# Reordered weight-row steps, an earlier value pass and one sink copy per pair in the first leg of a sink-window attention and squared-ReLU feed-forward kernel

## The chip, the core and the metric

The kernel runs on one core of a Trainium2 chip. The metric is the device time of one execution in microseconds (us). A core has TensorE (PE, with its weight loads PEld), VectorE (DVE), ScalarE (ACT), GpSimd (POOL) and SyncE (SP, which here only issues DMA transfers). Each engine works through its own instructions in the order in which they were written into its queue; semaphores make one engine wait for another.

## What is computed

```python
def _attn_ref(q, k, v, n_sink, window):          # 4 batches, 8 heads, 768 positions, head width 64
    scores = np.matmul(q, k.transpose(0, 1, 3, 2)) / np.sqrt(D)
    keep = is_sink | in_window                   # 4 sink keys and the last 128 keys
    scores = np.where(keep, scores, -1e9)
    a = np.exp(scores - scores.max(-1, keepdims=True))
    a = a / (a.sum(-1, keepdims=True) + 1e-9)
    return np.matmul(a, v)

def _moe_ref(x, w_in, w_out):                    # x: 3072 tokens x 512, from the heads above
    h = np.maximum(x @ w_in, 0.0)                # w_in 512 x 2048
    return h * h @ w_out                         # w_out 2048 x 512
```

The weights arrive as 64-bit floats and are split in the kernel into a high and a low part.

## The kernel before

The 3072 tokens are cut into 8 chunks of 384 (`c`), two to a batch. The 8 heads are taken as 4 pairs (`p`), so that a "pair" is one step of attention work for one chunk: `pairs` 0 to 3 belong to chunk 0, 4 to 7 (the fifth to the eighth) to chunk 1. For one pair the work is: `scores` (PE products `s`, a DVE pass at L263 that masks them and finds the maximum, an ACT exponential at L266), `normalise` (POOL, L291 to L305, which also packs the probabilities of the sink keys into `PSK`), `tail` (PE transposes the probabilities into PSUM tiles `pt`, and ACT or DVE copies them to `PTF`, L364 and L366; its middle step `sink_keys` transposes the sink probabilities into `pss` and copies them to `SK`, L325 and L326), and `values` (PE products `xo` from `PTF` and `SK`; ACT and DVE split the result into the high and low part of `x`, L418 and L419).

The feed-forward part (`moe`) runs in legs. For each of the 8 blocks of 128 hidden columns of a half leg it makes 12 products `ph` (L466) in two halves of 6, ACT applies ReLU and squares (L477, L480, L482), DVE forms the low part `gl` (L489), and one block later 9 products `po` follow (L504), three for each of three token tiles. It is written as a generator, and one call of `next(products)` is a quantum: half a block of `ph`, the other half, two thirds of `po`, the last third.

The weights come in 32 rows of 128 x 512 values. A row is loaded by SP into one of four buffers `raw` and then takes five steps in `split_steps`: `t` (DVE L569), a combination of `t` (DVE L571), `m` in two halves (ACT L573 and DVE L574), `eb` (DVE L576), and the two results (ACT L582 and DVE L583). `m`, `eb` and one of the temporaries have a single buffer each. The list `order` sets the order of rows: four rows of `w_in` ("i"), then four of `w_out` ("o"), and so on. A block of `ph` needs the four "i" rows of its quarter, a block of `po` the "o" row of its number.

In the first part of the program all queues are written by hand. There is a first stage (some 36 us) with the attention of the first four pairs and the start of the fifth, and then the first leg: 32 quanta (`QUANTA`), each of which takes one `next(products)`, one entry of the list `todo`, and `fill(k)`, that is k row steps. `todo` holds, for each of the pairs after the fifth, three entries of scores, one of `normalise`, one of `values` for the pair two before it, three steps of the `tail` of the pair before it, and one that loads `v`. The PSUM tiles of scores, `pt` and `pss` in this leg come from one pool of two buffers (`att`), so that each is written only when the one two before it has been read. 17 of the 32 rows are split by the end of the first leg (`EARLY`); the others follow in the second leg.

Of the kernel before, what the change touches and what calls it, by code (L numbers as in the profile page):

```python
# [19 lines left out]
P = 128  # L20
D = 64
NS = 8
# [3 lines left out]
NQ = TOK // P  # L26
WR = 512
SW = 64
# [9 lines left out]
def f32(ap):  # L38
    return ap.bitcast(F32)
# [3 lines left out]
def sink_window_attention_moe(  # L43
# [11 lines left out]
    nc = tc.nc  # L55
    B, NPAIR, _, S = q.shape
    H = 2 * NPAIR
    DM, FF = w_in.shape
    NCC = DM // P
# [9 lines left out]
    with ExitStack() as fast:  # L69
# [37 lines left out]
        ident = wp.tile([P, P], F32, name="ident")  # L107
# [45 lines left out]
        SK = wp.tile([P, TOK], F32R, name="SK")  # L153
# [38 lines left out]
        def load_v(c, p):  # L192
            st = state[c, p]
            st["vn"] = vn = ap2.tile([P, 4, 2, D], F32, tag="vn", name=f"vn_{c}_{p}")
            nc.sync.dma_start(
                out=vn[:, 0 : st["nk"]], in_=v[c // NHALF, p, :, st["kb0"] : st["kb0"] + st["nk"]]
            )
# [33 lines left out]
        def bank(tag, name):  # L231
            pool = {"att": ps_att, "h": ps_h, "xo": ps_x}.get(tag, ps_o)
            return pool.tile([P, 512], F32, tag=tag, name=name)
# [73 lines left out]
        def sink_keys(c, p, tag="att"):  # L307
            n = NQ - (1 if c % NHALF == 0 else 0)
            pss = bank(tag, f"pss_{c}_{p}")
            own = PSK[p % 2 if c < 2 else 0]  # L310
            if c > 1 and n == NQ:
                nc.tensor.transpose(pss[:, 0:P], f32(own[:, 0:2]).rearrange("p a c -> p (a c)"), ident)
                for a in range(NQ):
                    cols = slice(a * P, (a + 1) * P)
                    nc.vector.tensor_copy(SK[0 : 4 * NS, cols], pss[4 * NS * a : 4 * NS * (a + 1), 0:P])
                    nc.scalar.copy(SK[4 * NS : 6 * NS, cols], pss[4 * NS * a : 4 * NS * a + 2 * NS, 0:P])
                return
            for a in range(0, n, 2):
                nc.tensor.transpose(  # L319
                    pss[:, a * SW : a * SW + P], f32(own[:, a : a + 2]).rearrange("p a c -> p (a c)"), ident  # L320
                )
            copy = nc.scalar.copy if c == 1 else nc.vector.tensor_copy
            blocks = lambda t: t.rearrange("p (a c) -> p a c", c=P)
            rows = slice(0, 6 * NS)
            copy(blocks(SK[rows, 0 : n * P])[:, 0:n:2], blocks(pss[rows, 0 : (n + 1) // 2 * P]))  # L325
            copy(SK[rows, P : 2 * P], pss[SW : SW + 6 * NS, 0:P])  # L326

        def banks_of(c, p):

# [92 lines left out]
        pairs = [(c, p) for c in range(NCHUNK) for p in range(NPAIR)]  # L422
# [117 lines left out]
        wout_rows = w_out.bitcast(I32).rearrange("(fc p) e -> p fc e", p=P)  # L540

        order = []
        for fq in range(NFQ):
            order += [("i", fq, cc) for cc in range(NCC)] + [("o", 0, 4 * fq + j) for j in range(4)]
        NROW = len(order)
        HALF = NROW // 2
        AHEAD = 2
# [72 lines left out]
        QUANTA = 4 * FH  # L620
        EARLY = HALF + 1
        with tc.manual_schedule(engines={E.PE, E.DVE, E.Activation, E.Pool, E.SP}):
            steps = row_steps()

            def fill(n):
                for _ in range(n):
                    if len(split) < EARLY:
                        next(steps)
# [11 lines left out]
            def tail(s, spare, own=("att",) * 3):  # L640

                a = pairs[s]
                probs(*a, 0, own[0])
                if s == 0:
                    busy(10)
                yield
                sink_keys(*a, spare)
                probs(*a, 1, own[1])
                yield
                probs(*a, 2, own[2])  # L650
                yield
# [13 lines left out]
            for s in range(NPAIR):  # L665
# [19 lines left out]
                if s > 0:  # L685
                    if s > 1:
                        load_v(*pairs[s])
                    t = tail(s - 1, "o2", (*trios[0], trios[1][0]))
# [10 lines left out]
            s = NPAIR  # L699
# [7 lines left out]
            t = tail(s - 1, "o2", (*trios[0], trios[1][0]))  # L707
# [11 lines left out]
            todo = []  # L719
            for s in range(NPAIR + 1, 2 * NPAIR + 1):  # L720
                if s < 2 * NPAIR:
                    todo += [lambda s=s: (s + 1 < 2 * NPAIR and load_qk(*pairs[s + 1]), scores(s, 0))]
                    todo += [lambda s=s, i=i: scores(s, i) for i in range(1, NQ)]
                    todo += [lambda s=s: normalise(*pairs[s], (0, 1))]
                else:
                    todo += [lambda: values(*pairs[s - 2])]
                if s > NPAIR + 1:
                    todo += [lambda s=s: values(*pairs[s - 2])] if s < 2 * NPAIR else []
                t = tail(s - 1, "att")
                todo += [lambda t=t: next(t)] * 3  # L730
                if s < 2 * NPAIR:
                    todo.append(lambda s=s: load_v(*pairs[s]))
            todo.append(lambda: values(*pairs[2 * NPAIR - 1]))
            for n in range(QUANTA):
                next(products)

                if todo:
                    todo.pop(0)()
                fill(2 if n < QUANTA // 2 or n % 4 == 0 or n >= QUANTA - 12 else 1)
                if n % 4 == 3 and n < QUANTA // 2:  # L740
                    fill(1)
            while len(split) < EARLY:
                next(steps)
            for f in todo:
# [273 lines left out]
```

## Time and profile before

| | us |
|---|---|
| median of 3 runs | 703.43 |
| lowest and highest of them | 703.38, 704.15 |
| time of the profiled execution | 703.99 |
| its span, first to last instruction | 702.1 |
| TensorE busy in the span | 684.5 (97%) |
| VectorE busy | 432.1 (62%) |
| ScalarE busy | 439.1 (63%) |
| GpSimd busy | 226.1 (32%) |
| mean granted TensorE clock, share of full speed | 0.997 |

The shares are averages over stages. TensorE's busy time counts pipelined products from start to modelled end, so a product that waits inside a group can be counted as busy; idle time in a timeline row stands in square brackets, with the engine and line that ended it. In a timeline, the time from one row's start to the next row's start on the same engine is what an instruction costs its queue.

### The profile page before, as it was taken

What the parts mean: (1) busy time and instruction counts of PE and PEld (TensorE: products, weight loads), DVE (VectorE), ACT (ScalarE), POOL (GpSimd) and SP (SyncE); (2) the same over time, 40 slices, a digit from 0 to 9 for tenths busy, and PEclk for the clock granted to TensorE, in tenths of its full rate; (3) what the DMA queues carried; (4) which work ended last, traced back from release to release, by engine and by line L of the source; (5) the groups of instructions that cost most, each with busy time, mean ns of one, the idle gap of its engine ahead of it and who ended that gap; (6) DMA issues with size and microseconds to landing.
All of it is one profiled execution on the core that took longest, in us unless ns stands there. A gap on an engine that the chain in (4) does not pass through costs nothing.

```text
span 702.1 us, 11728 instructions
## 1 busy us (share of the span) xinstructions
PE 684.5 (97%) x3854; PEld 592.0 (84%) x3854; DVE 432.1 (62%) x1185; ACT 439.1 (63%) x1244; POOL 226.1 (32%) x433
## 2 busy tenths in 40 slices
PE   8889999999999999999999999999999999999995
PEld 4567889998888898888889888888888889889994
DVE  8988799835667665565566565666556665542221
ACT  6888887755666776776667777667677554422221
POOL 6664400034454432332342443233244242200000
PEclk9999999999999999999999999999999999999998
DMA  7575466412434333333434432243432210000001
GB/s 240 155 233 186 141 234 208 131 45 64 128 74 140 93 91 107 107 103 92 117 90 140 133 100 69 91 137 96 114 95 81 78 44 16 0 35 12 1 0 49
DMA packets 37027, 71.49 MB, mean 102 GB/s; under 512 B 4384, under 2 KB 14368, under 8 KB 36960
## 3 DMA queue, kind: packets, MB, share of 16 engines
q1 hardware_dynamic: 36816, 70.55, 34.1%
q8 instruction: 32, 0.52, 0.3%
q14 instruction: 35, 0.29, 0.1%
q10 hardware_dynamic: 144, 0.13, 0.1%
HBM read 62.80 MB, written 7.86 MB: 101 GB/s over the span
## 4 chain that ended last, share of the span: by engine, by line
PE 90%; ACT 4%; DVE 2%; issue 1%; POOL 1%; DMA 1%; SPq 0%; DVEq 0%; POOLq 0%; ACTq 0%
PE ph L466 37%; PE po L504 37%; PE xo L407 6%; PE s L259 5%; PE pt L377 2%; PE xo L410 2%; PE s L255 1%; ACT P L266 1%; ACT m L573 1%; PE pt L359 1%; DMA raw<-in_moe_w_in_dram 1%; POOL P L291 1%; ACT PTF L366 1%; DVE ob L527 0%; PE pss L319 0%
## 5 line engine op out<-in xcount | busy, mean ns | idle before, releaser
L466 PE MATMUL ph<-x,wi 128*128 128x384 f32 x1536 | 306.3, 340 | 0.6 <-ACT wi L582 0.4
L466 PEld LDWEIGHTS ph<-x,wi 128*128 128x128 f32 x1536 | 265.1, 188 | 10.3 <-issue 1.4
L504 PE MATMUL po<-wo,gh 128*128 128x512 f32 (+1 forms) x770 | 244.4, 398 | 0.0
L227 POOL TENSOR_TENSOR KS<-kn,KS 128x408 fp32r<-128x408 f32 (+1 forms) x48 | 58.2, 1213 | 320.2 <-ACT KS L226 320.2
L504 PEld LDWEIGHTS po<-wo,gh 128*128 128x128 f32 x770 | 136.0, 188 | 19.1 <-issue 1.6
L504 PE MATMUL po<-wo,gl 128*128 128x512 f32 x385 | 151.6, 394 | 0.0
L266 ACT ACTIVATE P<-P,nbs 128x264 f32<-128x264 f32 (+1 forms) x192 | 94.2, 491 | 75.1 <-DVE nbs L263 74.9
L485 DVE TENSOR_TENSOR ph<-ph,r 128x384 f32<-128x384 f32 x96 | 54.0, 563 | 76.8 <-ACT r L477 76.7
L263 DVE CUSTOM_DVE_ANT_0 P<-s,masks 128x264 f32<-128x264 f32 x160 | 67.2, 430 | 52.7 <-PE s L259 49.4
L291 POOL TENSOR_SCALAR P<-P,rs 128x136 f32<-128x136 f32 (+2 forms) x192 | 85.3, 459 | 31.4 <-DVE rs L280 29.5
L477 ACT ACTIVATE r<-ph 128x384 f32<-128x384 f32 x96 | 46.7, 487 | 77.7 <-PE ph L466 74.9
L489 DVE TENSOR_TENSOR gl<-ph,gh 128x384 fp32r<-128x384 f32 x128 | 71.1, 555 | 25.5 <-ACT ph L482 14.0
L504 PEld LDWEIGHTS po<-wo,gl 128*128 128x128 f32 x385 | 72.2, 188 | 16.0
L229 DVE TENSOR_TENSOR QS<-qn,QS 64x384 fp32r<-64x384 f32 x48 | 44.8, 933 | 24.4 <-ACT QS L228 23.9
L259 PE MATMUL s<-KS,QS 128*128 128x264 f32 (+1 forms) x288 | 57.2, 281 | 0.7 <-DVE nbs L263 0.7
L259 PEld LDWEIGHTS s<-KS,QS 128*128 128x128 f32 x288 | 51.9, 188 | 6.3 <-DVE nbs L263 1.5
L286 POOL TENSOR_TENSOR P<-P 128x256 f32<-128x256 f32 (+1 forms) x48 | 48.1, 1002 | 26.0 <-ACT P L266 25.5
L480 ACT ACTIVATE gh<-r 128x384 fp32r<-128x384 f32 x96 | 50.3, 524 | 2.2
L383 DVE TENSOR_TENSOR PTF<-pt,halves 128x256 f32<-128x256 f32 x96 | 36.2, 419 | 22.5 <-PE pt L377 21.9
L407 PE MATMUL xo<-PTF,vn 128*64 128x256 f32 (+1 forms) x448 | 46.5, 342 | 1.0 <-ACT PTF L366 1.0
L407 PEld LDWEIGHTS xo<-PTF,vn 128*64 128x64 f32 x448 | 31.2, 136 | 18.0 <-issue 9.3
L226 ACT CAST KS<-kn 128x408 fp32r<-128x408 f32 (+1 forms) x48 | 28.3, 589 | 26.7 <-issue 14.2
(107 smaller groups left out, 671.4 us busy)
## 6 DMA issues: line engine op xcount, KB each, us to landing
raw<-in_moe_w_in_dram SPq DMA_DIRECT2D x16, 512.0 KB, 3.8
raw<-in_moe_w_out_dram SPq DMA_DIRECT2D x16, 512.0 KB, 3.6
half<-in_moe_w_in_dram SPq DMA_DIRECT2D x32, 256.0 KB, 3.0
half<-in_moe_w_out_dram SPq DMA_DIRECT2D x32, 256.0 KB, 3.1
kn<-in_k_dram SPq DMA_DIRECT2D x24, 272.0 KB, 4.1
qn<-in_q_dram SPq DMA_DIRECT2D x32, 192.0 KB, 3.7
out_dram<-ob SPq DMA_DIRECT2D x23, 256.0 KB, 2.5
kn<-in_k_dram SPq DMA_DIRECT2D x24, 204.0 KB, 3.5
```

The costliest lines, as they stand in the source:

```text
L227: nc.gpsimd.tensor_tensor(KS[:, 1, 0:nk], st["kn"][:, hh, 0:nk], f32(KS[:, 0, 0:nk]), op=ALU.subtract)
L259: nc.tensor.matmul(ps[:, 0:n], st["QS", hh][:, qcols], flat[:, a, c0 : c0 + n], start=(a == 0), stop=(a == 1))
L263: nc.vector.tensor_tensor_reduce(Pt[:, i, 0:n], ps[:, 0:n], mask[:, 0:n], -SCALE, BIG, ALU.add, ALU.min, nb)
L266: nc.scalar.activation(Pt[:, i, 0:n], Pt[:, i, 0:n], AF.Exp, bias=nb, scale=-1.0, accum_out=sm[:, i : i + 1])
L286: nc.gpsimd.tensor_tensor(Pt[:, j0:NQ, 0:P], Pt[:, j0:NQ, 0:P], Pt[:, j0:NQ, BS:BAND], op=ALU.add)
L291: nc.gpsimd.tensor_scalar(Pt[:, j, 0:n], Pt[:, j, 0:n], rs[:, hh, j : j + 1], 1.0, op0=ALU.mult, op1=ALU.mult)
L407: nc.tensor.matmul(xo[h * D : h * D + D, cols], lhsT, rhs, start=(n == 0), stop=False, skip_group_check=True)
L466: nc.tensor.matmul(ph[:, 0:TOK], wi_at(i, cc, fc), xt[:, cc, :], start=(m == 0), stop=(m == 3 * NCC - 1),)
L480: nc.scalar.activation(gh, r, AF.Square)
L485: nc.vector.tensor_tensor(ph[:, 0:TOK], ph[:, 0:TOK], r, op=ALU.mult)
L489: late = lambda: nc.vector.tensor_tensor(gl, ph[:, 0:TOK], f32(gh), op=ALU.subtract)
L504: nc.tensor.matmul(po[t][:, e], gt[:, ts_], wo[f][:, i, e], start=(f == f0 and j == 0), stop=(f == f1 - 1 and j == 2), skip_group_check=True,)
```

## The change

Four edits. The sink transposes of chunks 0 and 1 are made one per token tile (two for each pair of chunk 0, three for each pair of chunk 1) instead of one per two tiles, and they land side by side in `pss`, so that one copy takes them to `SK` instead of two. The fourth "o" row moves behind the second quarter's four "i" rows in `order`. The load of `v` shares a `todo` entry with the third step of the `tail`, so that the entries behind it come one, two and three quanta earlier, and two empty entries stand ahead of the last `values`. And a table `STEPS` sets the row steps of quanta 2, 3, 6, 7 and 10 to 1, 0, 3, 5 and 3, where they were 2, 3, 2, 3 and 2; their sum, 12, is unchanged. For chunks from 2 on the copies of `sink_keys` are written differently but are the same instructions.

```diff
@@ sink_keys
-            if c > 1 and n == NQ:
+            rows = slice(0, 6 * NS)
+            if c < 2:
+
+                for a in range(n):
+                    nc.tensor.transpose(pss[0:SW, a * P : (a + 1) * P], f32(own[:, a]), ident)
+                (nc.scalar.copy if c == 1 else nc.vector.tensor_copy)(SK[rows, 0 : n * P], pss[rows, 0 : n * P])
+                return
+            if n == NQ:
...
-            for a in range(0, n, 2):
-                nc.tensor.transpose(
-                    pss[:, a * SW : a * SW + P], f32(own[:, a : a + 2]).rearrange("p a c -> p (a c)"), ident
-                )
-            copy = nc.scalar.copy if c == 1 else nc.vector.tensor_copy
...
-            copy(blocks(SK[rows, 0 : n * P])[:, 0:n:2], blocks(pss[rows, 0 : (n + 1) // 2 * P]))
-            copy(SK[rows, P : 2 * P], pss[SW : SW + 6 * NS, 0:P])
+            nc.tensor.transpose(pss[:, 0:P], f32(own[:, 0:2]).rearrange("p a c -> p (a c)"), ident)
+            for a in range(n):
+                nc.vector.tensor_copy(SK[rows, a * P : (a + 1) * P], pss[a * SW : a * SW + 6 * NS, 0:P])
@@ order
-            order += [("i", fq, cc) for cc in range(NCC)] + [("o", 0, 4 * fq + j) for j in range(4)]
+            order += [("i", fq, cc) for cc in range(NCC)]
+            order += [("o", 0, 4 * fq + j) for j in range(-1 if fq == 1 else 0, 3 if fq == 0 else 4)]
@@ first leg
-                todo += [lambda t=t: next(t)] * 3
-                if s < 2 * NPAIR:
-                    todo.append(lambda s=s: load_v(*pairs[s]))
-            todo.append(lambda: values(*pairs[2 * NPAIR - 1]))
+                todo += [lambda t=t: next(t)] * 2
+                todo.append(lambda s=s, t=t: (next(t), s < 2 * NPAIR and load_v(*pairs[s])))
+
+            todo += [lambda: None] * 2 + [lambda: values(*pairs[2 * NPAIR - 1])]
+            STEPS = {2: 1, 3: 0, 6: 3, 7: 5, 10: 3}
...
-                fill(2 if n < QUANTA // 2 or n % 4 == 0 or n >= QUANTA - 12 else 1)
-                if n % 4 == 3 and n < QUANTA // 2:
-                    fill(1)
+
+                fill(STEPS.get(n, 2 + (n % 4 == 3) if n < QUANTA // 2 else 2 if n % 4 == 0 or n >= QUANTA - 12 else 1))
```

On the chip's queues this stands as follows. DVE in the first stage, the tail of the third pair (`x`: the low part of the first pair's output of two pairs before; `SK`, `PTF`: the sink and probability copies; `wi`: a weight row's result), before:

```order
L576 TENSOR_SCALAR eb_460<-t_3_458 128x512
L419 TENSOR_TENSOR x_0_401<-xo_1_486,x_0_400 128x384
L325 CAST SK<-pss_2_506 48x128
L326 CAST SK<-pss_2_506 48x128
L364 COPY PTF_2_1_513<-pt_2_1_510 128x256
L583 SCALAR_TENSOR_TENSOR wi<-m_459,eb_460 128x512
L263 ISA P_0_0_532,nbs<-s_0_0_0_533,masks 128x264
```

and after:

```order
L579 TENSOR_SCALAR eb_460<-t_3_458 128x512
L420 TENSOR_TENSOR x_0_401<-xo_1_486,x_0_400 128x384
L316 CAST SK<-pss_2_506 48x256
L365 COPY PTF_2_1_513<-pt_2_1_510 128x256
L586 SCALAR_TENSOR_TENSOR wi<-m_459,eb_460 128x512
L263 ISA P_0_0_532,nbs<-s_0_0_0_533,masks 128x264
```

One copy has gone from between `x` and the copy to `PTF`; nothing else moved there.

ACT in the first leg, from the last exponentials of the sixth pair (`P_1`) over the tail of the fifth (`PTF_0`, `SK`) and the second feed-forward block (`ph_1`, `gh_1`), before:

```order
L266 ACTIVATE P_1_1_642,sm_1_636<-P_1_1_642,nbs 128x264
L582 CAST wo_687<-t_5_652 128x512
L573 COPY m_707<-raw_650 128x512
L366 COPY PTF_0_0_725<-pt_0_0_720 128x512
L582 CAST wo_728<-t_6_706 128x512
L477 ACTIVATE ph_1_713<-ph_1_713 128x384
L480 ACTIVATE gh_1_740<-ph_1_713 128x384
L482 ACTIVATE ph_1_713<-ph_1_713 128x384
L325 CAST SK<-pss_0_744 48x2x128
L326 CAST SK<-pss_0_744 48x128
L366 COPY PTF_0_1_754<-pt_0_1_749 128x512
L366 COPY PTF_0_2_775<-pt_0_2_770 128x512
```

and after:

```order
L266 ACTIVATE P_1_1_642,sm_1_636<-P_1_1_642,nbs 128x264
L367 COPY PTF_0_0_713<-pt_0_0_708 128x512
L585 CAST wo_715<-t_5_652 128x512
L478 ACTIVATE ph_1_701<-ph_1_701 128x384
L481 ACTIVATE gh_1_731<-ph_1_701 128x384
L483 ACTIVATE ph_1_701<-ph_1_701 128x384
L316 CAST SK<-pss_0_735 48x384
L367 COPY PTF_0_1_745<-pt_0_1_740 128x512
L576 COPY m_721<-raw_650 128x512
L367 COPY PTF_0_2_764<-pt_0_2_759 128x512
L585 CAST wo_769<-t_6_720 128x512
```

The first copy to `PTF` now stands ahead of a row's cast and of the next row's `m`; that `m` stands between the second and the third copy.

DVE from the last step of a row of `w_out` towards the second scores of the seventh pair (`P_2`), before:

```order
L583 SCALAR_TENSOR_TENSOR wo_786<-m_757,eb_758 128x512
L569 TENSOR_SCALAR t_8_791<-raw_731 128x512
L571 SCALAR_TENSOR_TENSOR t_8_791<-raw_731,t_8_791 128x512
L263 ISA P_2_0_809,nbs<-s_2_0_0_810,masks 128x264
L263 ISA nbs 128x1
L263 ISA P_2_1_814,nbs<-s_2_1_0_815,masks 128x264
L263 ISA nbs 128x1
L574 TENSOR_SCALAR m_792<-raw_731 128x512
L576 TENSOR_SCALAR eb_793<-t_8_791 128x512
L263 ISA P_2_0_809,nbs<-s_2_0_1_833,masks 128x264
```

and after:

```order
L586 SCALAR_TENSOR_TENSOR wo_769<-m_721,eb_722 128x512
L572 TENSOR_SCALAR t_7_774<-raw_718 128x512
L490 TENSOR_TENSOR gl_1_732<-ph_1_701,gh_1_731 128x384
L263 ISA P_2_0_788,nbs<-s_2_0_0_789,masks 128x264
L263 ISA nbs 128x1
L263 ISA P_2_1_793,nbs<-s_2_1_0_794,masks 128x264
L263 ISA nbs 128x1
L574 SCALAR_TENSOR_TENSOR t_7_774<-raw_718,t_7_774 128x512
L577 TENSOR_SCALAR m_775<-raw_718 128x512
L579 TENSOR_SCALAR eb_776<-t_7_774 128x512
L586 SCALAR_TENSOR_TENSOR wi<-m_775,eb_776 128x512
L572 TENSOR_SCALAR t_8_806<-raw_772 128x512
```

Between the first and the second scores of the seventh pair stand five row steps, where two stood before; the second scores' pass follows behind the last row shown.

## Rows read from the trace of the kernel before

**Rows 1.** Busy time by stretch: stretch; us, then PE, PEld, DVE, ACT, POOL busy.

```profile
0.00:36.00 36.00, 30.73 (x184) 18.21 (x184) 31.48 (x122) 26.31 (x81) 22.26 (x57) 1.00 0.68 199
...
44.00:94.30 50.30, 47.07 (x282) 36.36 (x281) 43.34 (x105) 42.34 (x99) 20.89 (x32) 1.00 0.56 174
...
131.00:702.10 571.10, 562.49 (x3166) 498.31 (x3164) 314.09 (x859) 335.46 (x993) 177.69 (x334) 1.00 0.29 82
```

**Rows 2.** PE's waits, 36 to 97 us: waiter, releaser, us, times, longest.

```profile
PE pt L359 <- ACT PTF L366: 1.4, 1, 1.4
PE xo L407 <- ACT PTF L366: 0.7, 1, 0.7
PE pt L359 <- ACT SK L326: 0.6, 1, 0.6
...
PE ph L466 <- ACT wi L582: 0.4, 1, 0.4
```

**Rows 3.** DVE's timeline, third pair's tail: start us, us, line, operation [idle before].

```profile
28.23 0.56 DVE L419 TENSOR_TENSOR x<-xo,x 128x384 fp32r<-128x384 f32 x1 [0.29 <-ACT x L418]
28.71 0.27 DVE L325 CAST SK<-pss 48x128 fp32r<-48x128 f32 x1
28.99 0.29 DVE L326 CAST SK<-pss 48x128 fp32r<-48x128 f32 x1
29.31 0.42 DVE L364 COPY PTF<-pt 128x256 f32<-128x256 f32 x1
29.66 0.68 DVE L583 SCALAR_TENSOR_TENSOR wi<-m,eb 128x512 fp32r<-128x512 int32 x1
```

**Rows 4.** PE's timeline at the end of the first stage.

```profile
34.20 1.88 PE L407 MATMUL xo<-PTF,vn 128*64 128x256 f32 x12 [0.31 <-ACT PTF L366]
```

**Rows 5.** ACT's timeline at the tail of the fifth pair.

```profile
44.15 0.60 ACT L582 CAST wo<-t 128x512 fp32r<-128x512 f32 x1
...
45.29 0.56 ACT L366 COPY PTF<-pt 128x512 f32<-128x512 f32 x1
...
46.56 0.47 ACT L477 ACTIVATE ph<-ph 128x384 f32<-128x384 f32 x1
...
47.86 0.37 ACT L325 CAST SK<-pss 48x256 fp32r<-48x256 f32 x1
48.24 0.26 ACT L326 CAST SK<-pss 48x128 fp32r<-48x128 f32 x1
...
49.73 0.80 ACT L573 COPY m<-raw 128x512 uint16<-128x512 uint16 x1
```

**Rows 6.** PE's timeline from the fifth pair's tail to the seventh pair's scores.

```profile
44.12 0.38 PE L319 MATMUL pss<-ident,PSK 128*128 128x128 f32 x2
45.91 0.66 PE L359 MATMUL pt<-ident,P 128*128 128x128 f32 x4 [1.40 <-ACT PTF L366]
46.32 0.71 PE L504 MATMUL po<-wo,gh 128*128 128x512 f32 x2
...
48.55 0.65 PE L359 MATMUL pt<-ident,P 128*128 128x128 f32 x4 [0.60 <-ACT SK L326]
...
50.90 0.71 PE L255 MATMUL s<-kn,qn 64*128 64x264 f32 x4
51.54 1.30 PE L466 MATMUL ph<-x,wi 128*128 128x384 f32 x6
52.78 1.03 PE L255 MATMUL s<-kn,qn 64*128 64x264 f32 x4
```

**Rows 7.** DVE's timeline around the seventh pair's first scores.

```profile
50.56 0.69 DVE L583 SCALAR_TENSOR_TENSOR wo<-m,eb 128x512 fp32r<-128x512 int32 x1 [0.30 <-ACT m L573]
51.17 0.44 DVE L569 TENSOR_SCALAR t<-raw 128x512 int32<-128x512 int32 x1
51.65 0.69 DVE L571 SCALAR_TENSOR_TENSOR t<-raw,t 128x512 int32<-128x512 int32 x1
52.26 0.43 DVE L263 CUSTOM_DVE_ANT_0 P<-s,masks 128x264 f32<-128x264 f32 x1
```

More of the change, by code (lines that the diff above doesn't have):

```diff
@@ L317, in sink_keys @@
                 return
-            for a in range(0, n, 2):
-                nc.tensor.transpose(
-                    pss[:, a * SW : a * SW + P], f32(own[:, a : a + 2]).rearrange("p a c -> p (a c)"), ident
-                )
-            copy = nc.scalar.copy if c == 1 else nc.vector.tensor_copy
-            blocks = lambda t: t.rearrange("p (a c) -> p a c", c=P)
-            rows = slice(0, 6 * NS)
-            copy(blocks(SK[rows, 0 : n * P])[:, 0:n:2], blocks(pss[rows, 0 : (n + 1) // 2 * P]))
-            copy(SK[rows, P : 2 * P], pss[SW : SW + 6 * NS, 0:P])
+            nc.tensor.transpose(pss[:, 0:P], f32(own[:, 0:2]).rearrange("p a c -> p (a c)"), ident)
+            for a in range(n):
+                nc.vector.tensor_copy(SK[rows, a * P : (a + 1) * P], pss[a * SW : a * SW + 6 * NS, 0:P])
         def banks_of(c, p):
```

## The prediction, written before the changed kernel was run

> **What bounds the kernel now.** I read the busy times by stretch first. From 131 us on TensorE (PE) is busy 562.5 of 571.1 us, and nothing in the change touches that part [rows 1]. Room is left in two stretches: in the first stage PE is busy 30.7 of 36 us while DVE is busy 31.5, and in the first leg (44 to 94.3 us) PE is busy 47.1 of 50.3 us with DVE at 43.3 and ACT at 42.3 [rows 1]. So a PE wait taken out of either stretch moves the end by as much, until DVE or ACT is late instead; they have only 7 and 8 us of slack in the leg. Second, I read whom PE waits for in the leg: 1.4 us for the copy to `PTF`, 0.6 for the sink copy, 0.4 for a weight row, 0.7 for a copy to `PTF` ahead of the last `values` [rows 2]. Third, the timelines around those waits. The first two are one place, the tail of the fifth pair: PE's second transposes wait for the first copy to `PTF`, the third for the sink copies [rows 6], and both copies stand on ACT behind row steps and ReLU [rows 5]. A fourth loss shows only as a long group: the seventh pair's second scores take 1.03 us where its first take 0.71 [rows 6], some 0.3.
>
> **One sink copy in the first stage.** The two DVE copies hold the queue from 28.71 to 29.31, 0.60 us, and the copy of 256 columns behind them holds it 0.35 (29.31 to 29.66) [rows 3]. One sink copy of 256 columns should cost that 0.35, so 0.25 goes at each of four pairs. It lies on the path: the `x` step ahead of it waits for ACT, whose work follows from the scores' DVE pass of the same round, and DVE then runs on without a gap through the copy and the row step to the next scores [rows 3]; and the last `values` of the stage takes 1.88 us, since its second product waits for a DVE copy behind the sink copies [rows 4]. The additional transpose costs 0.10 (four of them in 46.32 - 45.91 = 0.41 us [rows 6]); at the first pair it stands ahead of the copy and takes 0.1 of the gain, later DVE's wait for `x` hides it. Upper bound 4 x 0.25 = 1.0, lower 0 (if ACT or POOL, which I haven't followed here, set the pace). I take **-0.8**, near the top, because DVE is the busiest engine of the stage [rows 1].
>
> The Trainium skill (VectorE: DVE Perf Modes, the errata section) gives 120 + columns cycles at 0.96 GHz for a PSUM copy, by which two copies of 128 make 0.52 us and one of 256 0.39, and the term would be near -0.4; the rows' starts say 0.60 and 0.35, and I go by them.
>
> **The fifth pair's tail.** In the new order ACT's first copy to `PTF` takes the place of the cast at 44.15; it lasts 0.56, so PE starts its second transposes at 44.77 instead of 45.91 [rows 5, 6]. PE would be ready at about 44.6 (two transposes at 44.12, 0.38, and a third): 0.2 of wait stays. Then one cast (0.60, less the 0.1 by which ACT's instructions overlap), so ReLU starts near 45.15 instead of 46.56; ReLU and the squares take 1.30 (46.56 to 47.86), and the sink copy starts at 46.45. Its cost: 256 columns hold ACT 0.38 (47.86 to 48.24), 128 take 0.1 less, so 384 take 0.48 [rows 5]. PE's third transposes start near 47.0 instead of 48.55; PE is ready at 46.8 (0.41 and the two `po` groups' 1.63, from 46.32 to 48.55 less the 0.60 waited) [rows 6], another 0.2. Of 2.0 us, **1.6 goes**.
>
> **What is late next: the seventh pair's scores.** They now follow directly on the third transposes. Their second tile needs the buffer that ACT empties with the third copy, which now stands behind a row's `m`: 0.2. On DVE the row's last step needs that `m`: it starts 0.83 after it (49.73 to 50.56) [rows 5, 7]; `m` follows the sink copy and a copy to `PTF`, at 47.45, so DVE resumes at 48.3. From there its queue is fixed: last step 0.61, `t` 0.48, `gl` 0.48 (the `x` step of the same shape in rows 3), two score passes 0.7 (estimated from 0.43 each, overlapping a little), then five row steps of 0.61, 0.4, 0.4, 0.61, 0.48 (0.61 and 0.48 by starts; 0.4 estimated from the steps' spread), and one pass: 53.4 [rows 7]. PE from 47.0: transposes 0.41, `po` 0.8, scores 0.65, half a block 1.24, scores 0.65, half a block 1.24 [rows 6], and 0.2 of small waits: 52.2. Its third scores wait for the buffer that this DVE pass frees, **1.3** (bounds: 0, if DVE is as quick as in before, where two row steps stand there; 2.5, the five steps whole). Here five row steps have moved into one quantum. Behind PE's wait stands all its later work.
>
> **The rest of the leg.** The row steps' number is unchanged, so DVE's work is too. The "i" rows are done one row earlier, so the 0.4 for the row goes; the two empty entries put products ahead of the last `values`, so the 0.7 goes; the 0.3 in the seventh pair's scores is replaced by the waits above. Against that, one quantum less lies between each pair's `values` and its next tail, and ACT's sink copy of the sixth pair stands behind `m`, which waits for a DVE step, and behind ReLU: by the same reckoning PE's third transposes wait 0.5 there (bounds 0 and 1.4, the longest of this kind [rows 2]), and some 0.3 goes at the eighth pair's scores and later tails. Four additional transposes on a saturated PE: 4 x 0.10 = 0.4. On SP the `v` loads move ahead of a row's load, and one piece of the ninth pair's keys behind one; rows have four buffers and `v` is used pairs later, so I cost these at nothing. If the keys land late, ACT's cast of them holds up ReLU and the sink copy of the sixth pair, up to another 1.4.
>
> The Trainium skill (TensorE: Matmul & The Clock Gate, Part 4, PE-mode transpose) measures about 275 ns for a transpose, which speaks against this edit: the four would then cost 1.1 instead of 0.4 and the time would be 0.7 higher; the trace doesn't agree, since four in a row took 0.41 us [rows 6].
>
> **Sum.** Leg: gone 1.4 + 0.6 + 0.4 + 0.7 + 0.3 = 3.4; new 0.2 + 0.2 + 0.2 + 0.2 + 1.3 + 0.5 + 0.3 = 2.9, and 0.4 for transposes: -0.1, say -0.2 as some small waits will overlap. With the first stage -0.8: **-1.0**. The profiled execution took 703.99 with a span of 702.1, 0.56 above the median of 703.43; I take the difference against each: span 701.1, median **702.4**.
>
> **Rivals.**
> 1. The new waits don't come. DVE and ACT have slack in the leg as a whole; if row steps are quicker there or the passes are not last, the 1.3 and the 0.5 halve or vanish: 702.4 - 0.9 to -1.8, about 701.2. For it: before, row steps stood there too and cost PE 0.3. Against it: five, not two.
> 2. The first stage gives nothing: POOL's normalisation or ACT's exponentials set its rounds. Then 703.2. For it: DVE waits 0.29 for ACT in each round [rows 3]; against it: that ACT work itself follows from DVE.
> 3. DVE becomes the bound of the leg: the stall at the seventh pair's third scores recurs. It decides where DVE's steps between two scores cost more than PE's 1.9 (scores and half a block): five steps at 0.5 do, three would from 0.63 a step. If two more places pass it, at 1.3 each, 702.4 + 2.6 = 705.0, slower. Against it: between the other scores only two or three steps stand, at 0.4 to 0.61 [rows 7].
> 4. The additional transposes don't overlap their neighbours: two last 0.38 and four 0.66, so one alone lasts 0.24 [rows 6], and four on PE's path cost 1.0 instead of 0.4: 703.0. Against it: by starts, four take 0.41.
>
> **How the numbers follow.** About 0.2% (1.4 us) is what can be told from no change. Forecast 0.52, rival 1 0.24, rival 2 0.14, rival 3 0.06, rival 4 0.04. The likeliest is 702.4, within 0.2%. Its own spread (some 0.7 to either side, from the bounds of the 1.3 and the 0.5) has 0.08 below 702.0. Faster by over 0.2%: 0.24 + 0.08 = 0.32; slower: 0.05; within: 0.63. The range runs from 700.9 (most of rival 1) to 703.6 (rivals 2 and 4 included); rival 3 and the far end of rival 1 are left out.
>
> **What would show it.** First stage: PE's first block of `ph`, now after 36 us, starts 0.8 earlier. Fifth pair: PE's 1.4 and 0.6 shrink to 0.2 each. A new PE wait for DVE's score pass of over 1 us follows two quanta later; if it is missing, rival 1 holds. Sixth pair: a wait of about 0.5 at its third transposes, for the sink copy. The waits for the weight row and ahead of the last `values` are gone. The forecast is wrong if the first block doesn't come earlier, or if PE's waits in the leg sum to under 2 or over 4 us.

## The result, and the profile after

The changed kernel is slower: 706.84 us (median), against 704.15 for the kernel before, run beside it (seven runs; the 703.43 of the forecast is the median of three of them), a ratio of 1.0034 with a 95% interval of 1.0022 to 1.0046. The forecast was 1.0 us faster, with 0.05 for slower. The span of the profiled execution grew from 702.1 to 705.0 us, and the whole loss lies before 97 us.

The first block of `ph` tells the first stage from the leg. It starts at 36.44 us, where before it started at 36.23. The second leg's first block starts at 97.28, 60.84 later. In the kernel before that block was cut (three products ahead of 94.83, at 0.19 each), so that it began in effect 58.03 after the first. So the leg lost 2.8 and the first stage 0.2 (its first weight row landed 0.33 later in this execution). PE's rows for these blocks, before and then after:

```profile
36.23 1.20 PE L466 MATMUL ph<-x,wi 128*128 128x384 f32 x6
...
91.02 0.69 PE L466 MATMUL ph<-x,wi 128*128 128x384 f32 x3
...
94.83 1.75 PE L466 MATMUL ph<-x,wi 128*128 128x384 f32 x9
```

```profile
36.44 1.20 PE L467 MATMUL ph<-x,wi 128*128 128x384 f32 x6
...
97.28 2.28 PE L467 MATMUL ph<-x,wi 128*128 128x384 f32 x12
```

PE's waits from 36 to 100 us (waiter, releaser, us, times, longest), which answer to [rows 2]:

```profile
PE pt L360 <- ACT SK L316: 2.3, 2, 2.0
PE s L255 <- DVE nbs L263: 1.4, 2, 0.9
```

The 1.4 and 0.7 for copies to `PTF`, the 0.6 for the sink copy at the fifth pair and the 0.4 for the weight row are gone. What came is the forecast wait for DVE's score pass at the seventh pair (0.85 of the 1.4; the other 0.53 stood in the kernel before too) and one of 2.0 for the sixth pair's sink copy, where 0.5 was forecast. The changed kernel's ACT timeline shows what stood ahead of that copy; behind it stands the row of the same key cast in the kernel before:

```profile
60.14 0.59 ACT L367 COPY PTF<-pt 128x512 f32<-128x512 f32 x1 [0.34 <-PE pt L360]
62.39 0.54 ACT L226 CAST KS<-kn 128x408 fp32r<-128x408 f32 x1 [1.66 <-DMA kn<-in_k_dram]
62.83 0.76 ACT L576 COPY m<-raw 128x512 uint16<-128x512 uint16 x1
...
64.80 0.47 ACT L316 CAST SK<-pss 48x384 fp32r<-48x384 f32 x1
```

```profile
64.39 0.54 ACT L226 CAST KS<-kn 128x408 fp32r<-128x408 f32 x1
```

The cast of the ninth pair's keys, which used to run behind the sink copies without a wait, now stands ahead of `m`, ReLU and the sink copy, and waits 1.66 for a load. SP's queue in the changed kernel, and then in the kernel before, shows which:

```profile
54.90 0.65 SPq L187 DMA_DIRECT2D kn<-in_k_dram  x1
55.65 0.53 SPq L561 DMA_DIRECT2D raw<-in_moe_w_out_dram  x1
56.23 0.62 SPq L187 DMA_DIRECT2D kn<-in_k_dram  x1
```

```profile
56.48 1.31 SPq L187 DMA_DIRECT2D kn<-in_k_dram  x2
59.02 0.33 SPq L558 DMA_DIRECT2D raw<-in_moe_w_out_dram  x1
```

The second piece is issued earlier than before (56.2 instead of 57.2), and lands later (62.3 instead of 61.1): a weight row of 512 KB is ahead of it. Time from issue to landing of these two pieces, in the changed kernel and then in the kernel before:

```profile
DMA to landing us min/median/max: 4.3/5.2/6.1
```

```profile
DMA to landing us min/median/max: 3.9/4.0/4.0
```

PE lost more than the wait. Its own timeline, and busy times by stretch of 2 us (after the five engines stands the granted clock):

```profile
65.33 0.72 PE L360 MATMUL pt<-ident,P 128*128 128x128 f32 x4 [2.02 <-ACT SK L316]
65.74 1.16 PE L505 MATMUL po<-wo,gh 128*128 128x512 f32 x2
...
68.44 1.65 PE L467 MATMUL ph<-x,wi 128*128 128x384 f32 x6
```

```profile
64.00:66.00 2.00, 0.67 (x5) 0.68 (x6) 1.97 (x4) 2.00 (x5) 1.85 (x4) 0.95 0.67 219
66.00:68.00 2.00, 2.00 (x8) 1.02 (x6) 0.11 (x1) 0.75 (x2) 0.56 (x1) 0.50 0.16 55
68.00:70.00 2.00, 2.00 (x10) 1.33 (x6) 1.35 (x6) 0.87 (x3) 0.00 (x0) 0.70 0.00 0
```

Behind the idle time the granted clock is 0.50, the lower of its two levels (1.2 of 2.4 GHz); it rises again within the last slice, hence the 0.70. Two `po` products take 1.16 where [rows 6] has 0.71, and half a block of `ph` 1.65 instead of 1.30.

### The profile page after: what moved, and what is told of

Its sections match the earlier page's. It is cut to its first block, busy times and chain, and to the rows that moved or that the text cites. A ratio compares the mean times of both kernels' runs of the same rounds, so it can differ in the third digit from the quotient of the medians.

```text
span 705.0 us, 11731 instructions
## 1 busy us (share of the span) xinstructions
PE 686.5 (97%) x3862; PEld 593.5 (84%) x3862; DVE 429.4 (61%) x1181; ACT 438.1 (62%) x1240; POOL 228.5 (32%) x433
## 4 chain that ended last, share of the span: by engine, by line
PE 88%; ACT 4%; DVE 3%; POOL 2%; DMA 1%; issue 1%; SPq 0%; POOLq 0%; DVEq 0%; ACTq 0%
PE ph L467 37%; PE po L505 36%; PE xo L408 5%; PE s L259 5%; PE pt L378 2%; PE xo L411 1%; POOL P L291 1%; ACT P L266 1%; DMA kn<-in_k_dram 1%; PE s L255 1%; DMA raw<-in_moe_w_in_dram 1%; ACT m L576 1%; DVE P L263 1%; PE pt L360 1%; ACT ph L483 0%
## 5 line engine op out<-in xcount | busy, mean ns | idle before, releaser
L408 PE MATMUL xo<-PTF,vn 128*64 128x256 f32 x448 | 45.9, 342 | 0.2
```

The lines of the kernel that those rows point to most:

```text
L408: nc.tensor.matmul(xo[h * D : h * D + D, cols], lhsT, rhs, start=(n == 0), stop=False, skip_group_check=True)
```

## The experiments

Ratios are to the kernel before, run beside each; the last column is the time from the first block of `ph` to the second leg's first block, in the profiled execution. The runs were made on several chips, with medians of 704.15 to 704.96 for the kernel before, so rows are best compared by ratio and by leg. The leg repeats to 0.1 us (e6_steps and e15_again are the same kernel: 56.56 and 56.60), while the first stage's end moves between 36.0 and 38.1 from execution to execution. For e4_sinks_only, whose block is cut as in the kernel before, the two products ahead are taken off in the same way.

| kernel | median us | ratio, 95% interval | leg us |
|---|---|---|---|
| changed kernel | 706.84 | 1.0034, 1.0022 to 1.0046 | 60.84 |
| e1_cast_late | 704.67 | 1.0002, 0.9991 to 1.0012 | 58.49 |
| e10_keys_first | 704.42 | 0.9993, 0.9983 to 1.0003 | 58.42 |
| e2_fillers | 705.61 | 1.0018, 1.0007 to 1.0029 | 59.45 |
| e3_old_sinks | 708.36 | 1.0050, 1.0030 to 1.0069 | 61.79 |
| e4_sinks_only | 704.24 | 0.9995, 0.9984 to 1.0007 | 58.16 |
| e7_old_steps | 704.75 | 1.0004, 0.9996 to 1.0013 | 58.22 |
| e6_steps | 702.29 | 0.9969, 0.9959 to 0.9979 | 56.56 |
| e15_again | 702.66 | 0.9974, 0.9962 to 0.9987 | 56.60 |
| e12_steps8 | 702.14 | 0.9965, 0.9952 to 0.9978 | 57.01 |
| e11_old_sinks | 704.61 | 0.9996, 0.9985 to 1.0007 | 57.69 |
| e14_leg_old | 703.75 | 0.9995, 0.9984 to 1.0007 | 57.68 |
| e13_stage_old | 702.80 | 0.9975, 0.9965 to 0.9985 | 56.61 |
| e5_phase | 704.63 | 1.0008, 0.9998 to 1.0018 | 58.51 |
| e8_both | 702.29 | 0.9971, 0.9962 to 0.9980 | 56.63 |
| e9_warm | 704.10 | 0.9995, 0.9985 to 1.0005 | 56.56 |
| e16_fill | 702.48 | 0.9972, 0.9961 to 0.9984 | 56.61 |

### The key cast, its load and the clock

**e1_cast_late** writes the loads and the first key cast of the ninth pair into the leg's fixed order, where they had been left to the scheduler; SP's order stays, row 12's load between the two pieces included.

```diff
-                units += [lambda: start_pair(PAUSE), lambda: prep(PAUSE, 0), lambda: prep(PAUSE, 1)]
+                units += [lambda: None, lambda: prep(PAUSE, 0), lambda: prep(PAUSE, 1, "q")]
...
+                if n == 12:
+                    load_qk(*pairs[PAUSE])
                 if todo:
                     todo.pop(0)()
+                if n == 14:
+                    prep(PAUSE, 1, "k")
```

> The changed kernel with one instruction of ACT moved: the ninth pair's first key cast stands behind the sixth pair's third copy to PTF instead of ahead of m, ReLU and the sink copy; all other engines and SP's queue keep their order. Theory A (the loss is this cast's wait for its keys, 1.66 us on ACT, which becomes 2.02 us of PE waiting for the sink copy, and the low clock of the 3 us behind it, about 1.5 us more): the wait goes below 0.3, the granted clock stays at 1.00 between 62 and 70 us, and the time falls by 3.0 to 3.5, to 703.3 to 703.8. Theory A without the clock (the slow products have another cause): it falls by 2.0, to about 704.8. Theory B (row steps crowd DVE and ACT there, and the cast only fills a gap): PE waits over 1.5 us for the sink copy or for DVE's next score pass all the same, and the time stays above 706.

**e10_keys_first** leaves the cast where the changed kernel has it (`if n == 12: prep(PAUSE, 1, "k")`), and puts both pieces of the keys ahead of row 12's load.

> The changed kernel with one load of SP moved: the second piece of the ninth pair's keys stands ahead of the weight row's load again, as in the kernel before; the cast of the keys stays where the changed kernel has it, ahead of m, ReLU and the sink copy. Theory C (the piece behind a row's load is what makes the keys late): ACT's wait at the cast falls from 1.66 to 0.5 or less, the clock stays up, and the time is 704.5 to 705.2. Theory A (the place of the cast on ACT is what counts; the keys land too late for it in either order): the wait stays above 1.0 and the time above 705.8.

Either edit alone takes 2.4 us out of the leg, and the traces of both show no other change of order on ACT, SP or DVE in it. In e10_keys_first the pieces land 3.6 to 3.9 us after their issue, the cast doesn't wait, and PE's wait is down to 0.72. ACT's cast and PE's timeline there:

```profile
61.08 0.53 ACT L225 CAST KS<-kn 128x408 fp32r<-128x408 f32 x1
```

```profile
64.50 0.66 PE L362 MATMUL pt<-ident,P 128*128 128x128 f32 x4 [0.72 <-ACT SK L318]
64.91 0.71 PE L507 MATMUL po<-wo,gh 128*128 128x512 f32 x2
```

So of the theories on e10_keys_first C holds and A falls: the place on ACT costs only because the keys are late, and the keys are late because of one place in SP's queue. Theory B of e1_cast_late falls, though not whole: 0.7 of wait stays at the sink copy with or without the keys, and so the 3.0 to 3.5 forecast for that run was too much. Its 704.67 is near the 704.8 expected if the clock had no part, so the clock needed a run of its own. With either edit the kernel is as fast as the kernel before, not faster.

**e2_fillers** fills PE's idle time and leaves the wait for the keys.

```diff
+            if (c, p, bi) == (1, 1, 2):
+                fillers = bank("xo", "fillers")
+                for _ in range(9):
+                    nc.tensor.matmul(fillers[:, 0:TOK], wi_at(0, 0, 0), xT[0][0][:, 0, :], start=True, stop=True)
             pt = bank(tag, f"pt_{c}_{p}_{bi}")
```

> The changed kernel with nine additional products (384 columns each, results unused) in PE's queue ahead of the sixth pair's third transposes, where PE waits 2.02 us for the sink copy; the wait for the keys itself stays as it is. If PE's idle time brings the low clock: the clock stays at 1.00 behind the wait, the two po products take 0.71 again instead of 1.16 and the block of ph 1.3 instead of 1.65, and the time falls by 1.2 to 1.5, to 705.3 to 705.6, although PE's transposes start no earlier. If the low clock or the slow products come from something else, the time stays at 706.8, or rises by up to 0.2 for the products' tail.

```profile
63.10 1.75 PE L357 MATMUL fillers<-x,wi 128*128 128x384 f32 x9
65.05 0.66 PE L364 MATMUL pt<-ident,P 128*128 128x128 f32 x4 [0.20 <-ACT SK L316]
65.47 0.71 PE L509 MATMUL po<-wo,gh 128*128 128x512 f32 x2
```

The granted clock stays at 1.00 through 72 us, the leg is 1.4 shorter, and the time of 705.61 is at the forecast's 705.3 to 705.6. ACT's wait for the keys was 1.41 in this execution instead of 1.66, so some 1.1 of it is the clock. It is shown that PE's idle time brought the low clock: the same wait with unused products in it costs 1.1 less. Of the 2.4 us, then, 1.3 is PE's longer wait (2.02 less the 0.72 left) and 1.1 the clock behind it.

### The row steps of the leg

**e7_old_steps** is e1_cast_late with the fill rule of the kernel before (`STEPS = {}`), **e6_steps** with two of the seventh pair's five steps moved to the eighth pair's scores (the row loaded between the two pieces of keys is then row 11).

```diff
-            STEPS = {2: 1, 3: 0, 6: 3, 7: 5, 10: 3}
+            STEPS = {2: 1, 3: 0, 6: 3, 7: 3, 10: 3, 17: 2, 18: 2}
```

> e1_cast_late with the fill rule of the kernel before (no row step moved behind the fifth pair's copies; the values' loads, the row order, the sink copies and the last values as in the changed kernel). By the prediction's terms the fifth pair's waits come back (1.6 us), and the 1.2 at the seventh pair's scores (0.87 of waiting and 0.35 inside the group) goes: 704.9 to 705.3. Rival (the moved steps are a poor trade: what they give at the fifth pair they cost at the seventh, sixth and eighth): 704.3 or less.

> e1_cast_late with two of the five row steps of the seventh pair's first quantum moved to the eighth pair's last two score quanta (7: 3, and 17 and 18: 2). If the wait at the seventh pair's third scores comes from the five steps, as the prediction has it, PE's 0.87 for the score pass there goes to under 0.2 and, if nothing new is late, the time falls by 0.6 to 1.0 against e1_cast_late, to about 703.8. Rival (DVE is behind anyway, since it is busy without a gap from 58 to 66 us): the wait only moves to the sixth pair's tail or to the eighth pair's scores, and the time stays within 0.3 of e1_cast_late's.

PE's waits from 36 to 100 us in e1_cast_late, and then in e6_steps:

```profile
PE s L259 <- DVE nbs L267: 1.6, 3, 0.9
PE pt L364 <- ACT SK L320: 1.0, 2, 0.8
PE xo L412 <- ACT PTF L371: 0.2, 1, 0.2
```

```profile
PE po L509 <- ACT wo L589: 0.6, 1, 0.6
PE s L259 <- DVE nbs L267: 0.5, 1, 0.5
PE pt L364 <- ACT SK L320: 0.4, 2, 0.2
PE xo L412 <- ACT PTF L371: 0.2, 1, 0.2
```

The moved steps as the change has them are worth nothing: e7_old_steps has a leg 0.3 shorter, and a time that can't be told from e1_cast_late's (704.75, a little under its forecast). Its waits of 1.29 and 0.42 at the fifth pair are back, and in return nothing waits at the seventh. With three steps in place of five both are had: the wait at the seventh pair's third scores is gone, and so are the 0.76 at the sixth pair's sink copy and the 0.2 at the eighth pair's scores, with two row steps fewer ahead of both places on DVE and ACT; the leg is 1.9 shorter, where the forecast had counted the seventh pair alone, 0.6 to 1.0. A new wait of 0.6 for a weight row's cast is the price. e6_steps, and again e15_again, is 0.3% faster than the kernel before, and the version that beats both.

**e12_steps8** (`8: 3, 17: 2` instead of `17: 2, 18: 2`) was to take that 0.6 away.

> e6_steps with one of its two moved row steps back at the seventh pair's second scores (8: 3, 17: 2), since PE there waited 0.58 for a weight row's cast near 68.6 us. If three steps between two scores still hide: that wait goes and the time is 701.6 to 702.0. Rival (three steps are late for the third scores, or the sixth pair's sink copy is late again): a wait of 0.3 or more comes back at 53 or 63 us, 702.3 to 702.8.

The wait stayed at 0.59, the leg grew by 0.4, and the time can't be told from e6_steps. The forecast of 701.6 to 702.0 failed.

### The sink copies

**e4_sinks_only** is the kernel before with the sink edit alone, **e3_old_sinks** the changed kernel without it, **e11_old_sinks** e6_steps without it.

> The kernel before with the sink edit alone (one copy a pair, a transpose for each tile). The prediction's first-stage term: 704.15 - 0.8 + 0.3 for transposes, 703.6. Theory A (POOL's PSK cast takes it back at the end of the stage): 704.0 to 704.3, and PE's wait for PSK at the fourth pair grows by about 0.5 as it did in the changed kernel. In the leg the key cast stands one copy earlier than in the kernel before; if its keys aren't there by then, PE waits for a PTF copy there and the time is higher by that wait.

> The changed kernel with the sink edit undone (two copies a pair, transposes in twos), all moves kept, the key cast where the changed kernel has it. Theory A (the sink edit gave next to nothing: the first stage's gain was eaten by POOL's PSK cast at its end): 706.5 to 707.2. Rival (the sink edit gave the predicted 0.8 and only the later start of the first load hid it): 707.4 to 707.7. Rival (the additional transposes cost more than the copies give): 706.0 to 706.4.

> e6_steps with the sink edit undone (two copies a pair, transposes in twos): the worth of the sink edit where neither the key cast nor the five row steps disturb. By the rows so far it gives ACT 0.1 to 0.2 at each of the leg's four pairs and costs PE 0.11 there for the transpose, and in the first stage gives 0.1 to 0.7: with it undone 702.3 to 703.0. By the prediction's terms (0.8 less 0.4 for the transposes): 702.7. Rival (the transposes cost what the copies give): 702.1 to 702.3.

Alone the edit gives nothing, in time (0.9995) or in the leg (58.16 against 58.03). Undone in the changed order it costs: 61.79 instead of 60.84 in the changed kernel's leg, 57.69 instead of 56.56 in e6_steps'. The ratios are 1.0050 against 1.0034, with intervals that overlap, and 0.9996 against 0.9969; both times, 708.36 and 704.61, lie above what the theories had. To part the two places, **e13_stage_old** undoes it for `c == 0`, **e14_leg_old** for `c == 1`, both in e6_steps, with **e15_again** beside them.

> e6_steps with the sink edit undone in the first stage alone (two DVE copies a pair there). The prediction's term: 0.8 slower than e15_again. Theory A (POOL's PSK cast takes back all but a little): 0.1 to 0.3 slower. Theory D (the first stage's length differs from run to run by more than the edit does, with the start of the first load and the clock): within 0.2 of e15_again, with overlapping runs.

> e6_steps with the sink edit undone in the leg alone (two ACT copies a pair, transposes in twos). From the first block of ph to the first block of the second leg e11_old_sinks took 57.69, e6_steps 56.56: by that 1.0 to 1.2 slower than e15_again. By the prediction's terms (a copy of 384 columns for 0.48 in place of 0.38 + 0.26, less 0.10 of transposes): within 0.4 of it.

> e6_steps unchanged, as the base of the two runs before it: 702.3, and faster than the kernel before by 0.2 to 0.4%.

The first stage earns 0.14 (702.80 against 702.66), less than can be told from nothing. The leg earns 1.1, both in time (703.75 against 702.66) and in the leg's length (57.68 against 56.60). PE's waits in e14_leg_old, to hold against those of e6_steps above:

```profile
PE pt L374 <- ACT SK L324: 1.1, 3, 0.5
...
PE xo L422 <- ACT PTF L381: 0.4, 1, 0.4
PE pt L374 <- ACT PTF L381: 0.3, 1, 0.3
```

The second sink copy is paid at the third transposes of three pairs (1.1 instead of 0.4), and at a copy to `PTF` that stands behind it on ACT, ahead of the seventh pair's `values` (0.4 instead of 0.2). The 0.3 in the last row shown is no price of it: that copy to `PTF` stands ahead of the fifth pair's sink copies, and PE comes to it sooner by the transpose that it doesn't make. In all PE waits 1.0 more and its score groups take 0.4 longer, while four transposes less give 0.4 back. In the order before, PE waited for a sink copy at the fifth pair alone [rows 2]; in the changed order with two copies it does at three pairs, which fits that the edit earns something here and nothing there.

### Why the first stage gave nothing

**e5_phase** moves the first stage's row steps by one place, so that a row's last step no longer meets POOL's `PSK` cast; **e8_both** does so in e6_steps.

```diff
                     next(t)
-                else:
-                    fill(1)
...
             rest()
-            fill(1)
+            fill(2)
```

> The kernel with the late key cast (e1_cast_late), with the row steps of the first stage moved by one place: the first pair has one step less, the stage's end one more, so that a row's last step (DVE, two inputs from SBUF) no longer stands right ahead of the next pair's scores, where it ran beside POOL's PSK cast. Theory A (POOL's cast is held up by DVE's two-input step, and that is where the first stage's gain went): POOL's PSK casts near 23.4 and 29.4 take 0.2 instead of 0.92, PE's wait for PSK at the fourth pair goes from 0.9 to under 0.3, the first block of ph starts 0.5 to 0.9 earlier, and the time is 703.8 to 704.2 where e1_cast_late had 704.7. Rival (POOL's casts are slow for another reason, such as where the copies to PTF stand): they stay above 0.5 and the time stays within 0.3 of e1_cast_late's.

> e5_phase and e6_steps together, the version that should beat both kernels if both theories hold: 703.0 to 703.5, against 704.24 for the kernel before. If only one of them holds, 703.8 to 704.2; if neither, 704.7.

What they start from, in the changed kernel: POOL's cast and DVE's step at the fourth pair, PE's wait behind them, and the same cast in the kernel before.

```profile
29.37 0.93 POOL L304 CAST PSK<-P 128x32 fp32r<-128x32 f32 x1
```

```profile
29.55 0.67 DVE L586 SCALAR_TENSOR_TENSOR wi<-m,eb 128x512 fp32r<-128x512 int32 x1
```

```profile
33.24 0.41 PE L315 MATMUL pss<-ident,PSK 128*64 128x128 f32 x2 [0.87 <-POOL PSK L305]
```

```profile
29.19 0.21 POOL L304 CAST PSK<-P 128x32 fp32r<-128x32 f32 x1
```

In e5_phase and e8_both the casts are short again (0.21 and 0.28 at those places) and PE's 0.87 is 0.30 and gone. Yet the time is that of e1_cast_late and e6_steps: e5_phase's forecast of 703.8 to 704.2 failed, and e8_both lies under its 703.0 to 703.5 only because e6_steps does. In e8_both POOL's normalisation of the third pair's second head now takes 2.30 instead of 1.46, so the step had met another instruction of POOL's; and PE's clock was low from 24 to 28 us, behind two waits for copies to `PTF`. **e9_warm** and **e16_fill** put unused products ahead of those waits in e8_both, the one in the sink transposes' bank, the other in the first score's own:

```diff
             ps = bank(tag, f"s_{c}_{p}_{hh}_{i}")
+            if (c, p, hh, i) == (0, 3, 0, 0):
+                for _ in range(4):
+                    nc.tensor.matmul(ps, idle[:, 0:P], idle, start=True, stop=True)
```

> e8_both (row steps of the first stage moved by one place, two row steps of the leg moved) with five products whose results are unused in PE's queue ahead of the fourth pair's scores, where PE waited for copies to PTF (0.71 and 0.30) and its granted clock then stood at 0.50 to 0.70 from 24 to 28 us. If PE's idle time brought that low clock: the clock stays at 1.00 there, the xo products behind it take 1.30 instead of 2.25, the first block of ph starts 0.8 to 1.5 earlier than in e8_both, and the time is 700.8 to 701.6. Rival (DVE and POOL set the rounds, PE's slow products only fill its slack): the clock is back and the block starts within 0.3 of e8_both's; 702.0 to 702.5.

> e8_both with four products, their results unused, ahead of the fourth pair's first score product and in the same bank, so that they wait for nothing new. If PE's idle time near 22 us brings the clock of 0.50 to 0.70 from 24 to 28 us: the clock stays at 1.00, the xo products there take 1.30 instead of 2.25, and the time is 0.8 to 1.5 under e8_both's 702.3, 700.8 to 701.5. If not, or if the products only move the scores back: 702.0 to 703.0.

In e9_warm the products themselves waited 1.04 for the sink copy that had to leave their bank first, and the scores behind them came late: 704.10. That run says nothing on the clock's price. In e16_fill the clock stayed at 1.00. PE in e8_both and then in e16_fill:

```profile
24.61 2.25 PE L412 MATMUL xo<-PTF,vn 128*64 128x256 f32 x12
...
28.02 0.49 PE L319 MATMUL pss<-ident,PSK 128*64 128x128 f32 x2
```

```profile
24.70 1.30 PE L415 MATMUL xo<-PTF,vn 128*64 128x256 f32 x12
...
27.99 0.41 PE L322 MATMUL pss<-ident,PSK 128*64 128x128 f32 x2 [1.23 <-POOL PSK L312]
...
33.18 0.41 PE L322 MATMUL pss<-ident,PSK 128*64 128x128 f32 x2 [1.04 <-POOL PSK L312]
```

The products ran in 1.30 instead of 2.25, and what they won PE then spent waiting for POOL. The sink transposes start at 28.0 either way, and the time is the same, so the clock and the products came as forecast and the gain did not. That POOL sets the stage there is read from these waits; no run made POOL's own work shorter. Here the low clock cost nothing, since PE wasn't last; in the leg it cost 1.1, since it was.

## Why the prediction was wrong, point by point

**The piece of keys behind a row's load: the step that failed.** The prediction saw the move on SP and costed it at nothing, with "up to another 1.4" for late keys that went into no rival and no chance. It measured 2.4 (e10_keys_first undoes this alone). The path was the one that the prediction named, and its 1.4 is near the 1.3 by which PE's wait grew. Two things were missed. The argument for nothing, four row buffers and `v` used pairs later, covers the rows and `v`, not the keys, whose cast had moved ahead of the sink copy on ACT in the same change. And the price of a wait was taken as its length; the low clock behind it added 1.1.

**The first stage, -0.8.** Rival 2 came true in its outcome, with POOL for a part of the stage. The score passes show where the gain went: from round to round they took 7.00, 6.25 and 6.24 us before and 7.12, 5.98 and 5.96 after. So DVE did set the two later rounds, which gained the predicted 0.25 each. The first lost 0.1, and the stretch from the last of them to `ph` grew from 5.98 to 6.29. In both places DVE now has idle time in front of its scores, for PE:

```profile
18.21 0.29 DVE L263 CUSTOM_DVE_ANT_0 P<-s,mask 128x128 f32<-128x128 f32 x1 [0.26 <-PE s L255]
...
34.98 0.43 DVE L263 CUSTOM_DVE_ANT_0 P<-s,masks 128x264 f32<-128x264 f32 x1 [0.55 <-PE s L255]
```

PE in turn had waited there for POOL's `PSK`, 1.15 (as before) and the 0.87 above (nothing before). DVE without a gap in one round was no proof that it set them all. The trace of before could have told it: at the second pair POOL's cast took 0.56 beside the same DVE step, 0.21 at the same place of the next two. e13_stage_old puts the edit's worth in the stage at 0.14, which can't be told from nothing; no run shows what would have let the 0.8 through.

**The fifth pair, -1.6.** Right: its two waits are gone but for some 0.3.

**The seventh pair's third scores, 1.3.** Right in place and size: 0.85 of wait, and 0.35 inside a group that took 1.06 instead of 0.71. e6_steps shows the cause, the five row steps.

```profile
44.96 0.66 PE L360 MATMUL pt<-ident,P 128*128 128x128 f32 x4
...
53.42 1.06 PE L255 MATMUL s<-kn,qn 64*128 64x264 f32 x4 [0.85 <-DVE nbs L263]
```

**The sixth pair's third transposes, 0.5.** Near: 0.72 and 0.76 where the keys don't disturb (e10_keys_first, e1_cast_late).

**The weight row and the last `values`, -1.1.** Right: neither wait is left.

**Later places, 0.3.** Too small. In e1_cast_late the eighth pair's scores lose 0.2 in a wait and 0.55 inside two groups of 0.90 and 1.06, and the tails 0.15 and 0.25: 1.1. With the keys aside the leg is 0.4 longer than before (58.42 against 58.03), where the forecast had -0.2.

**The transposes, +0.4.** Right for themselves (three last 0.49, two 0.38), but e14_leg_old puts the leg's sink edit at -1.1, transposes included, in e6_steps' order. The copies' saving was counted at the fifth pair alone; with the steps moved, other pairs wait for a sink copy too. Only in the old order do copies and transposes cancel (e4_sinks_only).

Put together, the forecast of -1.0 missed 2.4 for the keys, some 0.8 in the first stage and 0.6 in the rest of the leg, 3.8 in all; the medians differ from it by 3.7. The chance of 0.05 for slower rested on rival 3, which didn't come: behind the seventh pair DVE's passes cost 0.2 in a wait (e1_cast_late), with no second stall of 1.3. No rival had the cause that made the kernel slower.

Of the signs named for a wrong forecast, the first block of `ph` told it (36.44, not 0.8 earlier). The sum of PE's waits in the leg did not: 3.7 us in the two rows at the top, inside the 2 to 4 named, since a low clock is in no wait.

## What to carry to other kernels

When a change lets a scheduler move a load or a cast, follow that instruction on every queue it passes: what stands ahead of the load on its DMA queue, what stands behind the cast on its engine, and who waits for that; a cost of nothing needs a reason for each of them. Where the granted clock falls behind a wait of a saturated PE, price the wait with that clock, and check by filling the gap with unused products. A stage in which one engine runs without gaps can still be set by another: before a term is put on the path, look at who releases the next stage's first wait.

## What the runs showed of the hardware

- A key piece with one load of 512 KB between it and the piece ahead landed 6.1 us after its issue (6.4 in e1_cast_late, 5.6 in e6_steps), without it 3.6 to 4.0 (e10_keys_first, the kernel before). The Trainium skill (DMA: Bandwidth & Descriptors, Queues, rings and completion order) says that each DMA engine takes a ring's descriptors in order; the landings agree, the row's at 61.4 (55.65 + 5.7) and the piece's behind it at 62.3.
- 2.0 us in which PE waited were followed by a granted clock of 0.50 for some 3 us, and with 1.75 us of products in them by 1.00. Not every wait does this: the 1.4 at the fifth pair in the kernel before [rows 6] was followed by 1.00 [rows 1].
- POOL's `PSK` cast takes 0.21 us at its shortest, and 0.54 to 0.93 where a DVE step with two inputs from SBUF runs beside it; it then ends 0.06 to 0.08 after that step (29.37 + 0.93 against 29.55 + 0.67). The Trainium skill (SBUF — State Buffer, Who interferes with whom) says that a DVE instruction with two SBUF inputs contends with a GpSimd instruction that reads SBUF, and calls the contention for the ports that they share an exclusive lock. The trace agrees in that the cast ends only behind the DVE step; its row starts ahead of the step's, so the trace doesn't show who had the lock. Nor does it show that the second input matters: beside DVE steps with one SBUF input the casts took 0.28 to 0.39 in the kernel before, and ended 0.07 behind them too (11.98 + 0.39 against 11.88 + 0.42).
